# Batched windowed attention with two feed-forward layers on one core: the corner of the v block buffer is cleared by an operation of its own, all band masks are added by TensorE, and the order table is new

## The chip, the cores and the metric

One core of one Trainium2 chip runs the whole program. The metric is the device time of one execution in microseconds (us). TensorE (PE in the profile, with PEld for its weight loads) multiplies matrices; VectorE (DVE), ScalarE (ACT) and GpSimd (POOL) do the elementwise work; SyncE (SP) issues nearly all transfers. Each engine takes its own instructions in the order in which the program lists them.

## What is computed

Attention over 4 batches, 8 heads, 576 positions and 64 columns: a path on inputs averaged over 4 positions, and a local path in which a position sees its neighbours at a distance under 4. Their sum, as 2304 tokens of 512 columns, goes through two feed-forward layers.

```python
def _attn_ref(q, k, v):                       # (4, 8, 576, 64) each
    ...
    out_d = sm_attn(q_d, k_d, v_d)            # q, k, v averaged over 4 positions
    out_up = np.repeat(out_d, factor, axis=2)
    mask = np.abs(pos[:, None] - pos[None, :]) < factor
    scores = scale * np.matmul(q, k.transpose(0, 1, 3, 2))
    scores = np.where(mask, scores, -1000000000.0)
    ...
    return (out_up + np.matmul(attn, v)).astype(np.float32)

def _moe_ref(x, w_in, w_out):                 # (2304, 512), (512, 2048), (2048, 512)
    h = x @ w_in
    return ((h * np.clip(h + 3.0, 0.0, 6.0) / 6.0) @ w_out).astype(np.float32)

def _moe2_ref(x, w1, w2, w3, w_out):          # three (512, 768), one (768, 512)
    return (np.maximum(np.maximum(x @ w1, x @ w2), x @ w3) @ w_out).astype(np.float32)
```

## The kernel before

**Arithmetic.** Activations and weights are split in two f16 parts (high and low), so that each product is three f16 matmuls. The weights come as 64-bit words. Each quarter of `w_in` and `w_out` (512 x 512) is read in two loads of 1 MB (L1152) into one of two raw buffers, and turned into f32 by one operation on ScalarE (L1124), one on GpSimd (L1126) and one on VectorE (L1129) per chunk; then it is squared and summed for a scale (L1169) and split (L1226 and L1228, for some chunks L1219, L1221 and L1223).

**Stages.** Attention of batch 0 opens the program, while the first quarter of the weights arrives. Then the first layer runs for batches 0 and 1 by quarters (`moe1_h`, L1267, and `moe1_y`, L1305), between the attention of batches 1 to 3. From about 340 us on come batches 2 and 3 of the first layer (L1430, L1521), the second layer's three products (L1842) and its output product (L1951), all with seven products in place of eight per block.

**Local attention of a half batch.** `local_scores` multiplies q and k in 12 blocks of 32 queries by 32 keys (L962), in six operations of 16 small matmuls into two PSUM banks. `soft` takes the softmax. For the pairs (batch, half) in `mask_pe` TensorE first writes the mask into the bank, by one bf16 matmul of an identity with `cap16` for each bank (L947), and VectorE reduces and subtracts straight from PSUM (L999, L1001). For the other pairs VectorE adds the mask (L1004, and L1006 for the edge block) into `sm`, reduces (L1008) and subtracts (L1010, on VectorE or GpSimd). `local_out` multiplies the transposed probabilities `pl` with `vw` (L1036), the block copy of v that `load_vw` fetches in eight transfers (L831), and L1056 adds the averaged path's `od` to make x. x is split by L640 (high, ScalarE) and L1340 (low), and the first layer's matmuls L1267 read it.

**The corner of `vw`.** The first block of batch 0 starts three rows before the first row of v, and the last block of batch 3 ends beyond the last. These blocks are cleared first: `load_vw` issues a GpSimd memset (L816 or L818) in the midst of the SP operation that issues the transfers, so that its place among GpSimd's instructions is the place of this SP operation in the order. The transfer of the shortened block (L824 or L828) waits for it, and on SP's queue all later transfers stand behind.

**Order.** `schedule` takes the operations in the order of a written-out table, `ORDER`: numbers are operations as they were recorded, an asterisk picks the other engine of those that can run on two, and `.1` puts in a warm-up matmul (L2085). The table thus sets each engine's sequence. Nothing else of the planner's constants (`FETCH` among them) is read when the program is built.

Of the kernel before, what the change touches and what calls it, by code (L numbers as in the profile page):

```python
# [64 lines left out]
 'mask_pe': ((0, 1), (1, 1), (2, 1), (3, 1), (3, 0)),  # L65
# [120 lines left out]
0-1 5 22 18 6 72 23 67 222 38 213 4 7 9-10 3 2 11-12 8* 19-20 15 13 74 16 24-26 14 27-28 32 34 33 21 69 29-30  # L186
35-36 43 17 44-45 71 31 37 86 88 98 87 89 46 75 99 76 100 77-78 47 79 48 93 90-91 39 92 94 80-81 101 95 68* 392
70* 49-50 73* 41 96* 97* 82-83 55-56 51 57-58 214 227 216 52* 105 219 231 103 40 102 226 110 113 160-161 104 223
215 111 59 115* 162 106-107 53 84 112* 218 109 119 108* 163 54 60 85 217 220 228 165 114 166 121* 120 167 164
224-225 116-117 122 172 61 118 62-64 168 229 221 173 247 123 65* 124 66 248 169 140 139 845 42 230 236 233 170  # L190
141 249-250 174-175 179 251-255 184 186 142 177 185 235 232 125 127 256 126 257 269 176 237 239 234 846 143-144
391 270 128 178 271 180 129 171 130 145 187 132 243 240 275 241 135 131 244-245 242 272 397 150-151 181 238 276
.1 246 188 146 189 258 136* 259 182* 183* 134 260 190 393 403 133 193 287 394 844 399 192* 194 191 137 147 273
398 152 195 261 395 859 262-266 196 402 197 267-268 278 280 198 274 138 400 295 288 281 296 148 289 297 149 847
282 153-154 290 285 283 401 291 408 155 277 279 156 298 860 405 292 157 299-300 404 303-304 293 158* 305 396 159
406 306-307 301 861 848 286 294* 199 862 201 849 308 311-312 200 313-314 409 309 540 302* 315 284 850-851 539
202-203 316 310* 410 317 319 856 852 320-321 863 853 209 318 322 210 .1 339 323 204-206 407 411 855 541 412 854
542 347 340 207 324-325 348 326-327 208 413 858 211-212 329 857 414 341 349 415-418 342 419-422 328 343-344 350
865 868 351 345 864 423 352 870 355-356 334 357-358 363 330 424 335-336 331-332 364-365 346 867 926 366 425 543
353 426 428 866 359 869 429 874-875 333 360 354* 433-436 427 928 927 929 361 367-368 877 545 337 371-372 441 930  # L200
437 906 871 442 932 338 551 369 547 876 362* 438-439 546 933 872 430 550 370* 908 548 907 449-450 443-444 451
445 878 452 376 373 377 556 912 931 934 873 374 431 453 552 375 544 935 446-447 882-887 936* 910* 894 888-889
895 440 457 378-379 381-382 458-460 432 890 380 553 448* 549 454 909 461 386-387 938 891* 950 383-384 487-489
896 462 940 939 455 941 456* 937* 952 554 880 879 557-558 897 388 490 943 495-497 944 892 385 945 491 953 498
389 942 463 898 559 946-947 899 492 390 499 464* 949* 948* 560 465 1000 466 493 951 555 471 893 503 472 500 1002
900-901 1001 1003-1005 501 561 902* 511 904 955 473-474 467-468 512 502* 913* 504 494* 562 505 513 506 1006 469
954 1007 903 563-565 475 911 905 507 980-981 566-572 508 1008 956 958* 509 573 914 477-479 959 480 1476 881 482
# [141 lines left out]
class Plan:  # L349
# [66 lines left out]
def kernel(  # L416
# [73 lines left out]
    T = {}  # L490
# [1635 lines left out]
```

## Time and profile before

| | |
|---|---|
| Median of 3 runs | 780.24 us (779.95 to 783.92) |
| Profiled execution | 780.03 us |
| Its span in the trace | 778.2 us |
| TensorE busy | 737.7 us, 95% of the span |
| VectorE, ScalarE, GpSimd busy | 564.5, 467.8 and 294.2 us |
| Transfers | 68.43 MB |

The profiled execution lies 1.83 us above its own span, and 0.21 us under the median. The page's strip of 40 slices shows TensorE at five to seven tenths in the first three slices (some 58 us), seven in the sixth, and nine in nearly all others; the granted clock falls to five and six tenths in the second and third slice. A share of busy time says little here: what counts is the front of the program, where TensorE waits, and which wait ends last there.

### The profile page before, as it was taken

How to read it: one execution, taken by the hardware profiler on the slowest of the kernel's cores; microseconds unless marked ns; L12 is line 12 of the kernel's file. 1: busy time of each engine (PE TensorE's matmuls, PEld its weight loads, DVE VectorE, ACT ScalarE, POOL GpSimd, SP SyncE). 2: the span in 40 equal slices, each digit the busy share in tenths (PEclk: the TensorE clock that was granted, in tenths of full speed). 3: DMA queues.
4: the chain of work that ended last, by engine and by line, in shares of the span. 5: the costliest groups of instructions: out<-in, count | busy, mean ns of one | idle time of the engine just before them, and what ended most of it. 6: DMA issues, size and time to landing. Idle time of an engine off the chain costs nothing.

```text
span 778.2 us, 20629 instructions
## 1 busy us (share of the span) xinstructions
PE 737.7 (95%) x8493; PEld 552.5 (71%) x8493; DVE 564.5 (73%) x1151; ACT 467.8 (60%) x1067; POOL 294.2 (38%) x325
## 2 busy tenths in 40 slices
PE   5658979999999999999999999999999999999998
PEld 4456756877777787777777777775556766676667
DVE  2959958767876678878954688469999558953793
ACT  5658859776656644549964687369826432633153
POOL 5636345557534223554232122123665402400060
PEclk9658999999999999999999999999999999999999
DMA  9495746741544000004566433204100100010002
GB/s 293 75 271 185 188 118 134 227 99 29 117 92 116 3 3 3 1 21 113 154 165 170 133 108 104 96 5 174 67 1 1 52 4 29 1 41 1 28 15 82
DMA packets 81248, 68.43 MB, mean 88 GB/s; under 512 B 56962, under 2 KB 68226, under 8 KB 81154
## 3 DMA queue, kind: packets, MB, share of 16 engines
q1 hardware_dynamic: 81154, 67.12, 30.8%
q8 instruction: 66, 1.08, 0.6%
q14 instruction: 28, 0.23, 0.1%
HBM read 56.10 MB, written 11.01 MB: 86 GB/s over the span
## 4 chain that ended last, share of the span: by engine, by line
PE 76%; DVE 4%; ACT 2%; issue 2%; POOL 1%; DVEq 0%; POOLq 0%; ACTq 0%
PE y L1521 12%; PE a L1842 10%; PE y L1842 9%; PE y L1305 8%; PE h L1267 8%; PE at L1951 7%; PE a L1430 6%; PE h L1842 3%; PE y L1430 3%; PE at L1036 2%; PE h L1430 2%; PE a L962 1%; PE at L922 1%; PE at L760 1%; PE a L1951 1%
## 5 line engine op out<-in xcount | busy, mean ns | idle before, releaser
L1267 PE MATMUL h<-x,wi 128*128 128x288 f16 x768 | 116.0, 290 | 2.7 <-DVE gf L1282 2.4
L1305 PE MATMUL y<-g,wo 128*128 128x288 f16 x768 | 114.1, 288 | 1.6 <-ACT y L1316 1.3
L1842 PEld LDWEIGHTS <-m2ow 128*128 128x128 f16 x756 | 73.9, 98 | 50.3 <-issue 2.0
L1521 PE MATMUL y<-ga,wo 128*128 128x288 f16 x768 | 96.9, 286 | 0.0
L1267 PEld LDWEIGHTS <-wi 128*128 128x128 f16 x768 | 73.5, 99 | 23.1 <-issue 4.0
L1305 PEld LDWEIGHTS <-wo 128*128 128x128 f16 x768 | 73.7, 98 | 21.5 <-issue 2.9
L1521 PEld LDWEIGHTS <-wo 128*128 128x128 f16 x768 | 75.0, 98 | 19.1
L1287 POOL TENSOR_TENSOR g<-gf,g 128x288 f16<-128x288 f32 x38 | 33.0, 870 | 59.4 <-ACT g L1285 56.7
L1842 PEld LDWEIGHTS <-m2w 128*128 128x128 f16 x378 | 36.9, 98 | 22.2
L1126 POOL TENSOR_SCALAR z<-z 128x384 int32<-128x384 uint32 (+1 forms) x36 | 22.5, 626 | 69.1 <-DMA z<-in_moe_w_dram 29.7
L1842 PE MATMUL a<-yb,m2ow 128*128 128x384 f16 x234 | 42.9, 326 | 1.6 <-DVE a L1852 0.9
L1430 PEld LDWEIGHTS <-S 128*128 128x128 f16 x384 | 37.5, 98 | 9.4
L1842 PE MATMUL y<-yb,m2ow 128*128 128x384 f16 x234 | 43.1, 326 | 0.0
L1129 DVE SCALAR_TENSOR_TENSOR zo<-zo,z 128x384 int32<-128x384 int32 (+1 forms) x36 | 22.9, 639 | 22.1 <-ACT zo L1124 10.8
L1285 ACT CAST g<-gf 128x288 f16<-128x288 f32 x64 | 27.0, 427 | 15.6 <-DVE gf L1282 14.7
L1951 PEld LDWEIGHTS <-hm 128*128 128x128 f16 x324 | 31.7, 98 | 6.1 <-issue 0.6
L1951 PE MATMUL at<-m2fw,hm 128*128 128x256 f16 x288 | 35.2, 272 | 0.7 <-DVE sc L626 0.3
L1430 PEld LDWEIGHTS <-wi 128*128 128x128 f16 x288 | 28.2, 98 | 7.1
L760 PE MATMUL at<-ident,stg 128*128 128x128 f32 x128 | 21.7, 313 | 8.2 <-DVE which L555 5.6
L1126 POOL TENSOR_SCALAR y<-y 128x1024 int32<-128x1024 uint32 (+1 forms) x20 | 22.3, 1114 | 18.0 <-DMA y<-in_moe_w_out_dram 15.4
L1430 PE MATMUL a<-x,S 128*128 128x288 f16 x192 | 28.6, 286 | 0.0
L1430 PE MATMUL y<-x,S 128*128 128x288 f16 x192 | 28.3, 286 | 0.0
(331 smaller groups left out, 1779.5 us busy)
## 6 DMA issues: line engine op xcount, KB each, us to landing
z<-in_moe_w_dram SPq DMA_DIRECT2D x24, 384.0 KB, 3.5
y<-in_moe_w_in_dram SPq DMA_DIRECT2D x8, 1024.0 KB, 6.0
y<-in_moe_w_out_dram SPq DMA_DIRECT2D x8, 1024.0 KB, 5.1
vw<-in_v_dram SPq DMA_DIRECT2D x62, 96.0 KB, 3.6
out_dram<-y SPq DMA_DIRECT2D x18, 256.0 KB, 2.1
stg<-in_k_dram SPq DMA_DIRECT2D x6, 512.0 KB, 6.8
stg<-in_q_dram SPq DMA_DIRECT2D x6, 512.0 KB, 5.7
stg<-in_v_dram SPq DMA_DIRECT2D x6, 512.0 KB, 3.9
```

The costliest lines, as they stand in the source:

```text
L760: nc.tensor.transpose(out=po[:, i, :, f], in_=T[n(f"{nm}{kc}{c // 2}")][:, f, 2 * (c % 2):2 * (c % 2) + 2, :], identity=ident[0:nr, 0:nr])
L1036: nc.tensor.matmul(out=T[pts[cc]][64 * hl:64 * hl + 64, i * QB:i * QB + QB], lhsT=T[n(f"vw{half}")][32 * c:32 * c + 32, i, hl, :], rhs=T[n ...
L1126: op("POOL", c_f32(n), prio, lambda: nc.gpsimd.tensor_scalar(out=words()[0], in0=words()[0].bitcast(U32), scalar1=0.8735 * 2.0 ** -29, sca ...
L1129: op("DVE", c_dve(n), prio, lambda: nc.vector.scalar_tensor_tensor(out=dst().bitcast(I32), in0=dst().bitcast(I32), scalar=3, in1=words()[0 ...
L1267: nc.tensor.matmul(out=hp(), lhsT=T[wt][:, a, kk, i * P:i * P + P], rhs=T[x16][:, e, kk, :], start=(kk == 0 and (a, e) == (0, 0)), stop=(k ...
L1285: op("ACT", c_act(CH, 0, False), prio + LEAD, lambda: nc.scalar.copy(out=T[g16][:, 0], in_=T[gf]), r=[gf], w=[(g16, 0)], new=[buf(g16, "ac ...
L1287: op("DVE", c_dve(CH), prio + LEAD, lambda e: e.tensor_tensor(out=T[g16][:, 1], in0=T[gf], in1=T[g16][:, 0], op=ALU.subtract), r=[gf, (g16 ...
L1305: nc.tensor.matmul(out=T[acc][:, 0:CH], lhsT=T[wt][:, a, i, d * P:d * P + P], rhs=T[gs[i]][:, e], start=(i == 0 and (a, e) == (0, 0)), sto ...
L1430: nc.tensor.matmul(out=ps_(x)(), lhsT=lhs(a, kt), rhs=T[xn][:, e, kt, :], start=(first and kt == 0 and (a, e) == (0, 0)), stop=(kt == 1 an ...
L1521: nc.tensor.matmul(out=T[acc][:, 0:CH], lhsT=T[wt][:, a, 2 * fb + i, d * P:d * P + P], rhs=hl[:, e * S + half * CH:e * S + half * CH + CH] ...
L1842: nc.tensor.matmul(out=b(to), lhsT=w_op(nm, o)[:, a, kt, fp * P:fp * P + P], rhs=T[f"yb{p}{y}"][:, e, kt, :], start=(first and kt == 0 and ...
L1951: nc.tensor.matmul(out=ps_(x)(), lhsT=h_op(p, fp, o)[:, a, i * P:i * P + P], rhs=T["m2wo"][:, j, e, fp, :], start=(first and fp == 0 and ( ...
```

## The change

- `load_vw`: the memset becomes a GpSimd operation of its own (L835 in the changed file), recorded ahead of the SP operation, which now waits for it as for any other. In the table it can thus stand anywhere ahead of the transfers. Lines after it move by two (L962 becomes L964, L1036 L1038, L1152 L1154, L1267 L1269).
- `mask_pe` holds all eight pairs; before it held five. New are half 0 of batches 0, 1 and 2. In half 0 of a masked pair, eight small score matmuls fall away (of 104), since no block overlaps its neighbour.
- `ORDER` is a new table. The numbers of the operations shift with the new ones, so nearly every row of it differs.
- `FETCH` is changed, but is not read.

```diff
- 'mask_pe': ((0, 1), (1, 1), (2, 1), (3, 1), (3, 0)),
+ 'mask_pe': tuple((b, h) for b in range(4) for h in range(2)),
...
-0-1 5 22 18 6 72 23 67 222 38 213 4 7 9-10 3 2 11-12 8* 19-20 15 13 74 16 24-26 14 27-28 32 34 33 21 69 29-30
...
+0-1 5 4 7* 11 9 42 3 12 10 18 22 6 69 23 19-21 64 8 210 15 38 24 219 43 16 25 13-14 29 2 31-32 136 34 30 26 33
...
-    FETCH = ((30.0, 6.0), (45.0, 4.2), (112.0, 3.6), (1e9, 3.0))
+    FETCH = ((30.0, 6.5), (45.0, 5.0), (130.0, 4.6), (1e9, 3.4))
...
-                if b == 0 and half == 0:
-                    nc.gpsimd.memset(vw[0:32, 0, 0, :], 0.0)
-                if b == B - 1 and half == 1:
-                    nc.gpsimd.memset(vw[96:128, 11, 1, :], 0.0)
...
-            op("SP", 6.0, prio, go, w=[t], new=[buf(t, "attn", f"vw{half}", [P, 12, 2, D])])
+            new, r = [buf(t, "attn", f"vw{half}", [P, 12, 2, D])], []
+            if (b, half) in ((0, 0), (B - 1, 1)):
+                r = [(t, "pad")]
+                op("POOL", 0.1, prio, lambda: nc.gpsimd.memset(
+                    T[t][96:128, 11, 1, :] if half else T[t][0:32, 0, 0, :], 0.0), w=r, new=new)
+                new = []
+            op("SP", 6.0, prio, go, r=r, w=[t], new=new)
```

Over the program the counts that change are few: TensorE gains six mask matmuls and loses 24 small score matmuls; VectorE loses six L1004, six L1006, six L1008 and two L1010, and GpSimd four L1010, for six L999 and six L1001 on VectorE. Of the low parts of g (L1287) 34 in place of 26 are on VectorE.

**SP's queue, from the first w_in loads to the first w_out loads.** `y_` is a raw weight buffer, `vw_561` is half 1 and `vw_572` half 0 of batch 0's block copy, `stg` batch 1's k. Before:

```order
L1152 DMA y_154<-in_moe_w_in_dram 128x2x512
L831 DMA vw_561<-in_v_dram 32x12x64 x8
L704 DMA stg<-in_k_dram 128x16x64
L824 DMA vw_572<-in_v_dram 29x64
L831 DMA vw_572<-in_v_dram 32x11x64
L831 DMA vw_572<-in_v_dram 32x12x64 x7
L1152 DMA y_583<-in_moe_w_out_dram 128x2x512
L1152 DMA y_698<-in_moe_w_out_dram 128x2x512
```

After, `vw_155` is half 0 and `vw_232` half 1:

```order
L1154 DMA y_199<-in_moe_w_in_dram 128x2x512
L820 DMA vw_155<-in_v_dram 29x64
L827 DMA vw_155<-in_v_dram 32x11x64
L827 DMA vw_155<-in_v_dram 32x12x64 x7
L827 DMA vw_232<-in_v_dram 32x12x64 x8
L1154 DMA y_539<-in_moe_w_out_dram 128x2x512
L1154 DMA y_590<-in_moe_w_out_dram 128x2x512
L704 DMA stg<-in_k_dram 128x16x64
```

Half 0 now comes first, ahead of half 1, and batch 1's k moves from between the halves to behind the w_out loads.

**GpSimd, the memset.** `pd` and `sm` are probabilities of the two paths, `qkd` the averaged q and k. Before:

```order
L881 TENSOR_TENSOR pd<-pd,dsm 72x288
L1126 TENSOR_SCALAR y_150<-y_150 128x512
L1019 TENSOR_TENSOR sm<-sm,mx 128x384
L816 MEMSET vw_572 32x64
L1126 TENSOR_SCALAR y_583<-y_583 128x512 x2
L1126 TENSOR_SCALAR y_698<-y_698 128x512 x2
```

After:

```order
L741 MEMSET qT 128x4x8
L742 MEMSET kT 128x4x3
L743 MEMSET kT 128x4x5
L835 MEMSET vw_155 32x64
L796 TENSOR_TENSOR qkd<-kT 128x2x2x16
```

The memset moves from behind the softmax of half 0 to the end of the constants.

**TensorE, from the first output blocks of the local path to the last.** `h<-pl,vw` is `local_out` of batch 0, half 0, 48 matmuls for each pair of heads' columns. Before:

```order
L1036 MATMUL h<-pl,vw_572 64x24 x48
L962 MATMUL y<-kT,qT 32x32 x32
L1036 MATMUL h<-pl,vw_572 64x24 x16
L962 MATMUL y<-kT,qT 32x32 x16
L891 MATMUL at<-ident,pd 128x72 x2
L893 MATMUL at<-ident,pd 32x72
L1036 MATMUL h<-pl,vw_572 64x24 x32
L2085 MATMUL h<-warm 128x224
```

After:

```order
L1038 MATMUL h<-pl,vw_155 64x24 x32
L615 MATMUL at<-tiny,ones 128x1
L1038 MATMUL h<-pl,vw_155 64x24 x16
L949 LDWEIGHTS id_85
L949 MATMUL y<-cap_84,id_85 128x384
L949 LDWEIGHTS id_85
L949 MATMUL y<-cap_84,id_85 128x384
L964 MATMUL y<-kT,qT 32x32 x48
L893 MATMUL at<-ident,pd 128x72 x2
L895 MATMUL at<-ident,pd 32x72
L964 MATMUL y<-kT,qT 32x32 x16
L893 MATMUL at<-ident,pd 128x72 x2
```

The first 48 output blocks now stand ahead of the masks and scores of half 1 (`y<-kT,qT`) instead of among them; the warm-up matmul that stood behind the last of them stands ahead of this piece.

## Rows read from the trace of the kernel before

**Rows 1.** Page, busy us (share of the span) xinstructions.
```profile
PE 737.7 (95%) x8493; PEld 552.5 (71%) x8493; DVE 564.5 (73%) x1151; ACT 467.8 (60%) x1067; POOL 294.2 (38%) x325
```

**Rows 2.** By stretch: busy us (count) per engine, PEclk, DMA share, GB/s.
```profile
20.00:40.00 20.00, 13.66 (x260) 9.41 (x257) 18.08 (x53) 13.25 (x49) 11.69 (x15) 0.62 0.47 74
40.00:60.00 20.00, 12.07 (x338) 9.48 (x337) 11.32 (x30) 11.08 (x27) 7.42 (x11) 0.50 0.90 269
```

**Rows 3.** By stretch, longer ones, same columns.
```profile
140.00:340.00 200.00, 196.93 (x3465) 156.68 (x3464) 150.91 (x356) 120.68 (x318) 94.95 (x110) 1.00 0.27 62
...
540.00:600.00 60.00, 58.44 (x362) 35.17 (x361) 57.87 (x96) 36.60 (x62) 33.30 (x21) 1.00 0.08 27
```

**Rows 4.** SP's waits, 0 to 140 us: in total, times, longest.
```profile
SPq L824 <- POOL vw L816: 15.1, 1, 15.1
```

**Rows 5.** Timeline of SP: start, us, what; transfers by line.
```profile
10.40 10.34 SPq L831 DMA_DIRECT2D vw<-in_v_dram  x8
...
36.72 0.30 SPq L824 DMA_DIRECT2D vw<-in_v_dram  x1
...
41.95 0.93 SPq L1152 DMA_DIRECT2D y<-in_moe_w_out_dram  x2
```

**Rows 6.** Timeline of GpSimd: start, us, what, count, [idle before <-releaser].
```profile
4.45 0.12 POOL L743 MEMSET kT<- 128x20 f32 x1
...
36.52 0.17 POOL L816 MEMSET vw<- 32x64 f32 x1
47.56 1.88 POOL L1126 TENSOR_SCALAR y<-y 128x512 int32<-128x512 uint32 x2 [10.87 <-DMA y<-in_moe_w_out_dram]
```

**Rows 7.** Timeline of TensorE, front of the program.
```profile
43.94 2.76 PE L1036 MATMUL h<-pl,vw 32*64 32x24 f32 x94 [2.82 <-DMA vw<-in_v_dram]
...
51.31 1.55 PE L1036 MATMUL h<-pl,vw 32*64 32x24 f32 x32 [3.78 <-DVE x L1056]
...
63.03 3.40 PE L1267 MATMUL h<-x,wi 128*128 128x288 f16 x15
```

**Rows 8.** Timeline of VectorE, front of the program.
```profile
25.28 0.56 DVE L1004 TENSOR_TENSOR sm<-y,cap 128x384 f32<-128x384 f32 x1
...
32.31 2.48 DVE L1129 SCALAR_TENSOR_TENSOR wi<-wi,y 128x512 int32<-128x512 int32 x4
...
48.24 0.69 DVE L1129 SCALAR_TENSOR_TENSOR wo<-wo,y 128x512 int32<-128x512 int32 x1 [7.08 <-POOL y L1126]
...
50.74 0.51 DVE L1056 SCALAR_TENSOR_TENSOR x<-h,sc,od 128x288 f32<-128x288 f32 x1
```

**Rows 9.** TensorE's waits over the span: in total, times, longest.
```profile
PE a L962 <- issue: 6.2, 3, 4.4
```

**Rows 10.** Timeline of TensorE around a long wait for nothing shown.
```profile
101.08 1.51 PE L962 MATMUL a<-kT,qT 64*32 64x32 f32 x154
107.03 0.80 PE L962 MATMUL a<-kT,qT 64*32 64x32 f32 x54 [4.44 <-issue]
```

**Rows 11.** Timeline of TensorE, two such waits that follow.
```profile
166.42 1.08 PE L962 MATMUL a<-kT,qT 64*32 64x32 f32 x103 [1.04 <-issue]
...
169.37 0.59 PE L922 MATMUL at<-pT,vd 128*64 128x72 f32 x10
170.33 0.47 PE L922 MATMUL at<-pT,vd 128*64 128x72 f32 x6 [0.38 <-issue]
```

**Rows 12.** Page, DMA queues: packets, MB, share.
```profile
q8 instruction: 66, 1.08, 0.6%
```

**Rows 13.** Timeline of TensorE: mask matmuls, and expert matmuls at full clock.
```profile
37.66 0.84 PE L947 MATMUL y<-cap,id 128*128 128x384 bf16 x2
...
96.44 2.38 PE L1267 MATMUL h<-x,wi 128*128 128x288 f16 x18
...
127.69 0.50 PE L947 MATMUL a<-cap,id 128*128 128x384 bf16 x2
```

**Rows 14.** By stretch around 65 us, columns as in Rows 2.
```profile
67.00:68.00 1.00, 0.98 (x9) 0.65 (x8) 0.93 (x3) 0.96 (x4) 0.72 (x1) 1.00 0.83 201
```

More of the change, by code (lines that the diff above doesn't have):

```diff
@@ L185 @@
 ORDER = """
-0-1 5 22 18 6 72 23 67 222 38 213 4 7 9-10 3 2 11-12 8* 19-20 15 13 74 16 24-26 14 27-28 32 34 33 21 69 29-30
[L187 to L205, printed above, removed]
@@ new lines @@
+2118-2119 2218 2215 2441 2114 2442 2144 2130 2443 2145 2150 2223 2120 2220 2149 2134 2138 2135 2444 2154
+2151-2152 2214 2224 2226 2136 2225 2133 2140 2147 2155 2153 2221 2139 2450-2451 2445 2452 2156 2453 2446 2227
+2222 2141 2228 2230-2231 2233 2229 2142 2237-2238 2240 2137 2143 2157-2158 2232 2161 2234 2163 2159 2236 2162
+2454-2455 2244 2164 2160 2235 2165-2166 2456 2447 2239 2245 2247 2517 2241 2448 2457 2521 2242 2449 2243 2246
+2252 2248 2251 1467 1413 2458 2253 2250 2519 2249 2522 2254 2258-2259 2261 2260 2255 2523 2525 2262 2460-2464
@@ new lines @@
+2381 2666 2696-2697 2669 2686 2385 2671 2387 2386 2701 2699 2687 2672 2685 2720 2383 2388 2688 2702 2721 2706
+2722 2391 2689* 2690 2703 2691 2389 2420 2382 2704 2390 2398 2392 2707 2693 2394 2692 2694 2705 2709 2421 2393
+2695 2399 2401 2723-2724 2710 2395 2708 2728-2730 2713 2715 2725 2711 2422 2712 2714 2400 2731-2734 2402
+2716-2718 2726 2423 2735 2403 2396 2727 2397 2405 2404 2412 2736 2406-2408 2831 2424 2409 2413 2415 2410 2414
+2416 2411 2417-2418 2738-2740 2747-2748 2741 2749-2751 2742 2752 2743-2746 2795 2836 2796 2801 2832* 2803 2833
@@ new lines @@
+2834* 2425-2426 2516 2430 2835 2838 2427-2428 2737 2429 2840 2839 2753 2797 3229 2754 2799 2755 2841 2757 2804
+2758-2761 2842-2844 2798 2802 2809 2805 2762-2764 2766 2800 2765 2767 3230 2768 2807 2806 2808 2845 2776
+2810-2812 2777 2769-2771 2778 2846-2847 2849 3231 2850 2779 3232 2813 2853 2780 2772-2774 2781-2783 2814 2848
+2815-2817 2756 2851 2785-2792 2818* 2784 2819 2431 2837 2820 2854 3233 2432 2934 2937 3234 2821 3235-3237 2855
+2935 2943 2775 2433-2434 2822 2940 2936 3240 2939 2793 3241 2794 2435 2865 2952 2856-2857 2950 2852 2436-2437
@@ new lines @@
+2858 2876 2859 2877* 2861 2860 2886 2862 2890 2863 2438-2439 2938 2942 2941 2944 2864 2887 2947 2891 2968
+2945-2946 2948-2949 2951 2874 2953 2956 2440 2959 2955 2966 2875* 2954 3551 2870 2957 2878 2866 2879 2961
+2880-2881 2867 2882 2894 2872 2868 2958 2960 2967 2888 2895* 2984 2970 2975 2871 2889 2963 2873 2883 2962 2965
+2884 2969 3001 2892 2964 2971 2982-2983 2885 2972-2973 2893* 2991 2974 2976-2977 2896 2995 2986 2978 2869 2898
+2979 2897* 2985 2899 2980 2988 3002 2900 2981 2908 2999 2987 2909 2989 2901* 2904 2993 2910 2912 2911 2914 3000
@@ new lines @@
+3147-3149 3130-3131 3123 3132-3133 3150 3152-3153 3155-3156 3134-3135 3157 3154 3159-3160 3136 3158 3137
+3164-3166 3161 3557-3558 3560 3162 3167 3297 3169-3170 3559 3171 3173-3175 3172 3563 3163 3168 3177-3179 3176
+3565 3180-3183 3185-3186 3184 3187 3280 3188 3292 3189-3191 3194-3197 3323 3192 3199-3201 3203-3204 3202
+3205-3206 3561-3562 3207-3213 3215-3217 3214 3218-3220 3224 3282 3567 3286 3285 3221 3225-3227 3284 3287 3291
+3293-3294 3304 3295-3296 3564 3298 3305 3299 3301 3313 3307-3308 3302 3310 3300 3317 3569 3309 3303 3311-3312
@@ L346 @@
+3822 3797 3771* 3826 3801 3798 3802 3827 3831-3832 3750* 3778 3780 3751 3779 3799 3781 3828 3803 3800 3833 3752
+3773 3784 3783 3804 3785-3786 3829 3805-3808 3834 3809-3810 3814-3816 3787 3811-3813 3839-3840 3817 3841 3830
+3842 3849-3851 3835-3837 3853-3855 3838 3844-3845 3852 3857 3856 3858-3863 3865 3818 3866-3867 3846 3864 3869
+3847 3868 3843 3848 3870-3878
 """
```

270 lines of the change are left out of this document (130 added, 140 removed).

## The prediction

> **What bounds the kernel now.** The reading starts with the busy times: TensorE is busy for 737.7 of 778.2 us [rows 1], so 40.5 us of idle time, plus what the half clock costs, is all that an order can win without less work. The stretches say where it lies. From 20 to 60 us TensorE is busy for 13.66 and 12.07 of 20 us, at a granted clock of 0.62 and 0.50 [rows 2]; that is 14.3 us. From 140 to 340 us it is idle for 3.1 us, and from 540 to 600 us for 1.6 us, with VectorE at 57.87 of 60 [rows 3]. So the front decides.
>
> There, one chain ends last. SP's queue stood for 15.1 us on the memset of the corner of `vw` [rows 4]: from 21.6 to 36.72 us, when the first transfer of half 0 left; the w_out loads, two places behind, left at 41.95 [rows 5]. GpSimd ran the memset at 36.52, though it had finished the constants at 4.57 (L743), and its next weight operation then waited 10.87 us for w_out [rows 6]. TensorE's local output stood from 41.12 to 43.94 for the `vw` transfer, a wait of 2.82, and its second part 3.78 us for VectorE's L1056 [rows 7]. VectorE reached that L1056 only at 50.74, because the w_out conversions L1129 stand ahead of it and waited 7.08 us [rows 8]. All of this is the same late queue, seen three times; only the last wait on the path counts, so the three are not added up. The expert matmuls' first long run begins at 63.03 [rows 7].
>
> **The change part by part.** *The memset.* Right behind L743 it runs at about 4.6 us, long before SP comes to it. Both halves' v transfers then fall in the time in which SP stood, and the w_out loads wait only for their raw buffers, which the four L1129 of w_in empty from 32.31 to 34.79 [rows 8]. They leave between 32.2 (first buffer emptied early) and 34.8 us in place of 41.95: 7.2 to 9.8 us earlier. Does the rest of the front follow? The local output's other inputs were there by 41.12, and it takes 2.76 us [rows 7], so its first part ends by 43.9 at the latest, and earlier now that it stands ahead of half 1's scores. L1056 can then run at 42 to 44 in place of 50.74: 6.8 to 8.7 us earlier. The splits of x and of w_in behind it keep their lengths. I take **-8** for the start of the long run. If another queue is as late, only TensorE's own 2.8 us go; the ends are -2.8 and -9.8. Half 0 now comes first on SP, where half 1's eight transfers took 10.34 us among the other loads [rows 5], so half 0 lands some 15 us before it is read. Batch 1's k, which moves behind the w_out loads, is not read before the long run, whose start ends its cover.
>
> *The new order around scores.* TensorE waited 6.2 us in three pieces, 4.4 the longest, for nothing that the profile shows ahead of the small score matmuls [rows 9]. The longest came after 154 of 208 such records in one run [rows 10]. Two later ones, at 166.42 and 170.33, have 128 matmul records between them (103, 12, 3 and 10 in four rows, the first and the last shown [rows 11]), and as many weight loads: 256 instructions. The instruction queue moved 1.08 MB in 66 packets, 16.4 KB each [rows 12]. I read these as waits for the next block of instructions, and dense small matmuls use up a block faster than the next one comes. In the new order the run of 104 score matmuls of batch 1, half 0 (two records each) is cut in two of 48 with fifteen expert matmuls between them, which at 132 ns each (2.38 us for 18 [rows 13]) lengthen the block by 2.0 us; the wait should shrink by as much. Elsewhere runs of 64 remain. I take **-2**; the ends are 0 and the whole -6.2.
>
> [...]
>
> *The masks.* Three more pairs of mask matmuls cost 0.84 us at the half clock (batch 0) and 0.50 each at the full one [rows 13], 1.84 in all. Of the small score matmuls 24 go, 48 records at 1.51 / 154 = 9.8 ns [rows 10], 0.47. TensorE's work grows by 1.4 us; the pair in the front partly lies beside waits, so **+1** (0 to +1.4). VectorE loses additions of 0.56 us (L1004 [rows 8]); behind the front these lie beside a busy TensorE and are worth nothing there. In the front they pull the w_in conversions ahead a little, which is in the span of 7.2 to 9.8.
>
> *Everything else that moved.* The low parts of g and the like change engines, and nearly each row has a new place. No row prices that. The idle time after 140 us in the two stretches is 3.1 + 1.6 = 4.7 us [rows 3], the most that could be won; as much may be lost. Value 0, ends -4.7 and +4.7.
>
> The sum: 780.03 - 8 - 2 + 1 + 0 = **771.0 us**. The profiled execution lies 0.2 us under the median, which changes nothing.
>
> **The rivals.** *The waits are not fetches.* Then cutting up the scores leaves them as they are, and the term is 0: 773.0 us. For it: the profile names no releaser. Against it: the spacing of 256. [...]
>
> *Another wait takes the place.* ScalarE and VectorE take their rows in order, and if a conversion or the half clock's small matmuls end as late as the queue did, only 2.8 us of the front go, and the dense front waits for instructions in its turn (no -2): 780.03 - 2.8 + 1 = 778.2 us, no change that can be told. For it: half 1's scores and outputs, some 190 small matmuls, now come back to back, and each block of instructions may then cost a wait like the 4.44. Against it: from 20 to 60 us TensorE ran 598 matmul records and 594 weight loads [rows 2], 4.7 blocks, which at 4.44 + 1.26 us each (the long wait and about what TensorE worked on that block) are 27 us of the 40.
>
> [...]
>
> *More is won.* Front at -9.8 and all of the 6.2: 780.03 - 9.8 - 6.2 + 1 = 765.0.
>
> **How the numbers follow.** The forecast, 771 give or take 4, has 0.54; waits that are not fetches 0.13; another wait 0.20; the slower clock 0.07; more won 0.06. A measurement of this kernel can tell about 0.5%, 3.9 us: faster means under 776.3, slower above 784.1. The forecast, the first and the last rival are faster, 0.73; another wait is no change, 0.20; 0.07 is slower. The range runs from 766 to 778.5: it takes in the forecast with its ends, the first rival and most of "another wait", and leaves out the slower clock and part of the ends.
>
> **What would show it.** Right: SP has no wait on GpSimd in the front; the w_out loads leave at 32 to 35 us; VectorE's wait ahead of the first w_out conversion is under 2 us; the first long run of expert matmuls begins at 54 to 57 us; TensorE's waits for nothing shown ahead of score matmuls sum to about 4 us, none near 4.4; TensorE is busy for about 739 us. Wrong in the front: the w_out loads leave early and the long run still begins after 60. Wrong in the second term: the waits keep their sum. Wrong in the last: TensorE idles for over 8 us after 140 us.

## The result and the profile after

The changed kernel takes 771.73 us (median of four, 769.71 to 773.87) against 780.41 for the kernel before (779.95 to 783.92): a ratio of 0.9876, 95% interval 0.9854 to 0.9898 (9.7 us by the ratio, 8.7 by the medians). The prediction was 771.0 us with 766 to 778.5. The profiled execution is the slowest of the four: 773.87 us, span 772.1. The total thus came out as forecast; the three terms that make it up did not, as the experiments show.

The page's busy time of each engine ([rows 1] before):

```profile
PE 734.2 (95%) x8451; PEld 550.4 (71%) x8451; DVE 557.0 (72%) x1142; ACT 472.4 (61%) x1079; POOL 280.9 (36%) x316
```

The stretches of [rows 2, 3]: length, busy us (count) of PE, PEld, DVE, ACT and POOL, granted clock, DMA share, GB/s:

```profile
40.00:60.00 20.00, 14.44 (x369) 11.33 (x364) 15.39 (x41) 14.58 (x31) 11.43 (x14) 0.50 0.73 196
...
140.00:340.00 200.00, 197.06 (x3455) 156.72 (x3454) 150.82 (x349) 120.05 (x320) 89.80 (x104) 1.00 0.21 52
...
540.00:600.00 60.00, 56.83 (x354) 34.41 (x352) 59.36 (x97) 34.36 (x62) 30.36 (x20) 1.00 0.02 8
```

The queue did what was forecast. SP's timeline (start, length, line; [rows 5]) has no wait for GpSimd ([rows 4]); the v transfers of both halves leave early, and the w_out loads at 32.84 us in place of 41.95:

```profile
12.22 17.55 SPq L827 DMA_DIRECT2D vw<-in_v_dram  x16
32.84 2.38 SPq L1154 DMA_DIRECT2D y<-in_moe_w_out_dram  x2
```

VectorE's timeline ([rows 8]) shows the step behind it: no wait ahead of the first w_out conversion (L1131), and the first L1058 (L1056 before) at 42.91 in place of 50.74. But its second pair begins only at 53.05:

```profile
40.95 2.04 DVE L1131 SCALAR_TENSOR_TENSOR wo<-wo,y 128x512 int32<-128x512 int32 x2
42.91 0.93 DVE L1058 SCALAR_TENSOR_TENSOR x<-h,sc,od 128x288 f32<-128x288 f32 x2
...
53.05 0.52 DVE L1058 SCALAR_TENSOR_TENSOR x<-h,sc,od 128x288 f32<-128x288 f32 x1 [0.71 <-PE h L1038]
```

Before, the second pair began at 57.66:

```profile
57.66 0.50 DVE L1056 SCALAR_TENSOR_TENSOR x<-h,sc,od 128x288 f32<-128x288 f32 x1
```

So the first pair comes 7.8 us earlier, the second only 4.6, and the long run moves like the second.

What stands between is on TensorE's timeline (start, length, line, shapes, count of records, idle time ahead and what ended it; [rows 7]), after half 1's masks:

```profile
26.00 0.45 PE L964 MATMUL y<-kT,qT 64*24 64x32 f32 x31 [3.78 <-issue]
...
41.24 0.81 PE L964 MATMUL y<-kT,qT 64*32 64x32 f32 x55
44.30 0.69 PE L964 MATMUL y<-kT,qT 64*32 64x32 f32 x41 [2.25 <-issue]
44.92 0.50 PE L893 MATMUL at<-ident,pd 72*128 72x72 f32 x2
45.22 0.32 PE L895 MATMUL at<-ident,pd 72*32 72x72 f32 x1
45.47 0.47 PE L964 MATMUL y<-kT,qT 64*32 64x32 f32 x32
45.87 0.50 PE L893 MATMUL at<-ident,pd 72*128 72x72 f32 x2
46.16 0.32 PE L895 MATMUL at<-ident,pd 72*32 72x72 f32 x1
46.42 0.76 PE L964 MATMUL y<-kT,qT 64*32 64x32 f32 x49
49.94 0.36 PE L964 MATMUL y<-kT,qT 64*32 64x32 f32 x15 [2.77 <-issue]
...
59.14 3.09 PE L1269 MATMUL h<-x,wi 128*128 128x288 f16 x12
```

The rows from 44.30 us to the wait that ends at 49.94 hold 41 + 2 + 1 + 32 + 2 + 1 + 49 = 128 records, with their loads 256 instructions: one block in 5.64 us, of which 2.77 were waited. The long run begins at 59.14, 3.9 us earlier than before, not at 54 to 57. TensorE's waits by line (in total, times, longest; [rows 9]) say the same: the waits for nothing shown have nearly left the a bank of batches 1 to 3, where they were 6.2 us, and stand in the front (the y bank), where they were 0.6. Ahead of score matmuls they sum to 9.7 us, where the forecast was about 4:

```profile
PE y L964 <- issue: 8.8, 3, 3.8
...
PE a L964 <- issue: 0.9, 3, 0.5
```

### The profile page after: what moved, and what is told of

It is laid out like the page before. It is cut to its first block, busy times and chain, and to the rows that moved or that the text cites. A ratio compares the mean times of both kernels' runs of the same rounds, so it can differ in the third digit from the quotient of the medians.

```text
span 772.1 us, 20559 instructions
## 1 busy us (share of the span) xinstructions
PE 734.2 (95%) x8451; PEld 550.4 (71%) x8451; DVE 557.0 (72%) x1142; ACT 472.4 (61%) x1079; POOL 280.9 (36%) x316
## 4 chain that ended last, share of the span: by engine, by line
PE 80%; DVE 10%; ACT 3%; DMA 3%; issue 3%; SPq 1%; DVEq 0%; ACTq 0%
PE y L1523 12%; PE y L1307 11%; PE h L1269 10%; PE a L1844 8%; PE y L1844 8%; PE at L1953 7%; PE a L1432 6%; PE y L1432 3%; PE h L1844 3%; PE at L1038 2%; DMA y<-in_moe_w_in_dram 2%; PE h L1432 2%; PE at L924 1%; PE a L964 1%; DMA wi<-in_k_dram 1%
## 5 line engine op out<-in xcount | busy, mean ns | idle before, releaser
L1269 PE MATMUL h<-x,wi 128*128 128x288 f16 x768 | 118.0, 292 | 1.1 <-DVE gf L1284 1.1
L1269 PEld LDWEIGHTS <-wi 128*128 128x128 f16 x768 | 74.6, 100 | 22.2 <-issue 2.6
L1289 POOL TENSOR_TENSOR g<-gf,g 128x288 f16<-128x288 f32 x30 | 23.5, 785 | 55.0 <-ACT g L1287 54.8
L1131 DVE SCALAR_TENSOR_TENSOR zo<-zo,z 128x384 int32<-128x384 int32 (+1 forms) x36 | 18.7, 520 | 24.5 <-ACT zo L1126 23.0
L1287 ACT CAST g<-gf 128x288 f16<-128x288 f32 x64 | 26.9, 428 | 7.6 <-DVE gf L1284 5.9
L1280 ACT ACTIVATE r<-h,sc 128x288 f32<-128x288 f32 x32 | 18.7, 588 | 19.2 <-PE h L1269 19.0
L1342 POOL TENSOR_TENSOR m2fw<-hm 128x384 f32<-128x384 f32 x9 | 9.4, 1048 | 56.9 <-DVE hm L1858 56.4
```

The lines of the kernel that those rows point to most:

```text
L1131: op("DVE", c_dve(n), prio, lambda: nc.vector.scalar_tensor_tensor(out=dst().bitcast(I32), in0=dst().bitcast(I32), scalar=3, in1=words()[0 ...
L1269: nc.tensor.matmul(out=hp(), lhsT=T[wt][:, a, kk, i * P:i * P + P], rhs=T[x16][:, e, kk, :], start=(kk == 0 and (a, e) == (0, 0)), stop=(k ...
L1280: op("ACT", c_act(CH, 2), prio + LEAD, lambda: nc.scalar.activation(out=T[r_], in_=hp(), func=AF.Relu, scale=col(INVH + 4 * b + g), bias=c ...
L1287: op("ACT", c_act(CH, 0, False), prio + LEAD, lambda: nc.scalar.copy(out=T[g16][:, 0], in_=T[gf]), r=[gf], w=[(g16, 0)], new=[buf(g16, "ac ...
L1289: op("DVE", c_dve(CH), prio + LEAD, lambda e: e.tensor_tensor(out=T[g16][:, 1], in0=T[gf], in1=T[g16][:, 0], op=ALU.subtract), r=[gf, (g16 ...
```

## The experiments

Each ratio is to the kernel before, run on the same chip beside it. The changed kernel was measured once, four executions against four, so a difference to it carries the intervals of both ratios. A shorter or longer table shifts the lines: L957, L1031 and L1262 in the kernel with the memset alone are L964, L1038 and L1269 of the changed one; L954, L1028 and L1259 in those with the masks alone or the scores cut are L962, L1036 and L1267 of before. "Long run" is the first long run of expert matmuls in the profiled execution.

| kernel | ratio, 95% interval | long run | span |
|---|---|---|---|
| before | 1 | 63.03 | 778.2 |
| memset alone | 0.9947 (0.9928 to 0.9965) | 61.65 | 777.2 |
| masks alone | 0.9965 (0.9948 to 0.9982) | 62.66 | 776.7 |
| masks alone, padded | 0.9997 (0.9984 to 1.0010) | | 779.9 |
| scores cut | 0.9994 (0.9976 to 1.0012) | 62.34 | 778.5 |
| changed, memset late | 0.9933 (0.9909 to 0.9958) | 61.97 | 776.5 |
| changed, without the masks | 0.9957 (0.9937 to 0.9977) | 62.59 | 777.5 |
| changed | 0.9876 (0.9854 to 0.9898) | 59.14 | 772.1 |
| changed, blocks shifted | 0.9892 (0.9846 to 0.9938) | 61.00 | 778.4 |
| changed, local output first | 0.9899 (0.9870 to 0.9928) | 56.90 | 770.4 |
| changed, mixed | 0.9997 (0.9974 to 1.0019) | 70.60 | 778.1 |

### The memset alone

The kernel before, with its own order; the memset of batch 0 is recorded ahead of the SP operation and stands behind the constants (later numbers shift by one).

```diff
-0-1 5 22 18 6 72 23 67 222 38 213 4 7 9-10 3 2
+0-1 5 22 18 6 73 23 68 223 38 214 4 42 7 9-10 3 2
...
-                if b == 0 and half == 0:
-                    nc.gpsimd.memset(vw[0:32, 0, 0, :], 0.0)
```

> The kernel before with one thing changed: the memset of the corner of batch 0's half-0 vw tile is a GpSimd operation of its own, right behind the constants of the first operation (L741 to L743). All other operations keep their row; half 1's eight v transfers still stand ahead of half 0's on SP. Theory of the prediction (one late queue, seen three times): SP loses its 15.1 us wait, the w_out loads leave near 33 us in place of 41.95, VectorE's 7.08 us wait ahead of the first w_out conversion shrinks to under 2, and the long run of expert matmuls begins 3 to 8 us earlier than 63.03; time 772 to 777 us. Theory from the trace after (dense small matmuls are paced by waits for instruction blocks): the same early loads, but the waits for nothing shown ahead of small matmuls between 20 and 60 us grow from 0.6 to several us, and the long run begins 2.8 to 4.5 us earlier; time 775.5 to 777.5. Rival (hidden anyway): under 1 us, 779 to 781.

Measured: 0.9947, 4.1 us of 780.4 (2.7 to 5.6). The w_out loads left at 34.53 and VectorE's wait fell to 0.59 us, yet the long run began only 1.4 us earlier, less than either of the first two theories had it. TensorE's timeline of this kernel, at the places of [rows 7]:

```profile
41.63 1.47 PE L1031 MATMUL h<-pl,vw 32*64 32x24 f32 x42
44.81 1.69 PE L1031 MATMUL h<-pl,vw 32*64 32x24 f32 x54 [1.71 <-issue]
46.43 0.89 PE L957 MATMUL y<-kT,qT 64*32 64x32 f32 x64
47.25 0.77 PE L1031 MATMUL h<-pl,vw 32*64 32x24 f32 x9
51.77 0.85 PE L1031 MATMUL h<-pl,vw 32*64 32x24 f32 x23 [3.74 <-issue]
```

The waits of 2.82 us for vw and 3.78 for L1056 are gone, and waits for nothing shown of 1.71 and 3.74 have come at nearly the same places, 127 recorded records apart (54 + 64 + 9). In the old order the rival "another wait takes the place" is what happened in the front.

### The memset late, in the new order

The changed kernel; the memset goes behind GpSimd's softmax product (62), half 1's transfers (136) go ahead of half 0's (43).

```diff
-0-1 5 4 7* 11 9 42 3 12 10 18 22 6 69 23 19-21 64 8 210 15 38 24 219 43 16 25 13-14 29 2 31-32 136 34
+0-1 5 4 7* 11 9 3 12 10 18 22 6 69 23 19-21 64 8 210 15 38 24 219 136 16 25 13-14 29 2 31-32 34
...
-62* 161
+62* 42-43 161
```

> The changed kernel with one thing undone: the memset stands behind GpSimd's softmax product of half 0, and half 1's v transfers stand ahead of half 0's on SP, as in the kernel before. Theory of the prediction (the queue decides): SP waits for the memset until about 35.5 us, the w_out loads leave at 40 to 42 us in place of 32.84, TensorE waits some 5 us for the vw transfer, and the long run begins 4 to 9 us later than 59.14; time 776 to 781. Theory that instruction blocks pace the front: part of the delay lies beside waits for blocks (8.8 us in the changed kernel's front), since a TensorE that stands for vw collects a block meanwhile: the long run begins 2 to 5 us later, time 774 to 777, and the waits for nothing shown ahead of batch 0's small matmuls fall below 5 us.

Measured: 0.9933. SP waited 12.3 us for the memset, the w_out loads left at 39.41, TensorE waited 0.74 and 3.54 us for vw, and the long run began at 61.97, 2.8 us later. The waits ahead of the y bank's scores were 5.8 us in place of 8.8: here a TensorE that stood for vw for 4.28 us waited 3.0 us less for blocks. By the ratio the time is 775.2 us of 780.4. That and the long run are as the second theory had them; its mark of waits below 5 us was missed by 0.8, and the first theory's 4 to 9 us for the long run did not come. Against the changed kernel the memset (with the order of v's halves) is worth 0.0057, 4.4 us (give or take 2.6, from both intervals), about half of the 8 of the forecast.

### Are the waits blocks of instructions?

The changed kernel with 16 tiny matmuls behind the first warm-up matmul:

```diff
+        warmed.append(0)
+        for _ in range(16 if len(warmed) == 1 else 0):
+            nc.tensor.matmul(out=T["tail"][0:32, CH:CH + 24], lhsT=warm[0:32, 0:32], rhs=warm[0:32, 0:24],
+                             start=True, stop=True)
```

> The changed kernel with 16 tiny matmuls (32 records, 64 instructions of TensorE with their weight loads) behind the first warm-up matmul near 31 us, where TensorE has room; the results go to unused columns. Theory that the waits for nothing shown in the front are waits for the next block of 256 instructions: the wait at 26.00 us stays where it is, and the two later ones move 32 records ahead: the one at 44.30, behind 55 records of half 1's scores, comes behind about 23, and the one at 49.94, behind 49 records of the last piece, behind about 17. Rival (the waits belong to the matmuls ahead of which they stand, for a bank or for data): they stay behind 55 and 49 records. Time within 1.5 us of the changed kernel's by both.

TensorE's timeline of this kernel, the same rows as above:

```profile
40.42 0.43 PE L964 MATMUL y<-kT,qT 64*32 64x32 f32 x23
42.89 1.02 PE L964 MATMUL y<-kT,qT 64*32 64x32 f32 x73 [2.04 <-issue]
...
45.34 0.37 PE L964 MATMUL y<-kT,qT 64*32 64x32 f32 x17
49.09 0.74 PE L964 MATMUL y<-kT,qT 64*32 64x32 f32 x47 [3.38 <-issue]
49.76 2.34 PE L1038 MATMUL h<-pl,vw 32*64 32x24 f32 x80
54.95 0.64 PE L1038 MATMUL h<-pl,vw 32*64 32x24 f32 x16 [2.84 <-issue]
```

The waits stand behind 23 and 17 records in place of 55 and 49, each 32 records earlier, ahead of matmuls that had waited for nothing. A wait that belonged to a bank or to data would have stayed. A third boundary now falls into L1038 and costs 2.84 us. The two blocks took 6.20 and 5.86 us. The ratio cannot be told from the changed kernel's. The profiled execution, the slowest of six with a span of 778.4 us, also has a wait of 2.31 us at 252.53 that the changed kernel's does not have; that where the boundaries fall is worth some us by itself is suggested by this, not shown.

What the waits are for can be read from the traces directly, which hold the packets of the instruction queue ([rows 12]) one by one. The changed kernel's wait from 47.18 to 49.94 us has one in it (a row of its DMA view for this stretch):

```profile
q8 instruction: 1, 0.02, 2.2%
```

It left at 47.52 and had landed at 48.49, and TensorE went on 1.45 us later. It is the same everywhere. In the 14 traces there are 69 waits for nothing shown of over 0.4 us. All of them stand at the same place modulo 256, within one, when TensorE's recorded instructions (matmuls, weight loads and semaphore operations) are counted from the start (193 or 194 stand ahead in the traces before and after), and each ended 1.3 to 1.7 us after a packet of 16,384 bytes on that queue had landed. So they are waits for the next block of instructions. The releaser that a view names can hide one: the changed kernel's wait of 2.19 us that ends at 124.24, put down to VectorE's L1001, stands at such a place behind 128 score records in one run and ended 1.5 us after a packet.

### A run of scores cut in two

The kernel before; three of the six score operations of batch 1, half 0 (882 to 887) go ahead.

```diff
-376 373 377 556 912 931 934 873 374 431 453 552 375 544 935 446-447 882-887
+376 882-884 373 377 556 912 931 934 873 374 431 453 552 375 544 935 446-447 885-887
```

> The kernel before with one thing changed: three of the six score operations of batch 1, half 0 stand twelve expert matmuls earlier, so the run of 104 score matmuls is cut in two. Theory that the waits for nothing shown are waits for the next block of instructions: the 4.4 us wait near 107 us falls to 0 to 2.5 us, the sum of such waits ahead of a<-kT,qT from 6.2 to 2 to 4.5, and the time to 776.5 to 779. Rival (the waits are not fetches): the sum stays at 6 to 6.5 us and the time within 779.5 to 781.

TensorE's timeline, to be read beside [rows 10]:

```profile
99.24 1.36 PE L954 MATMUL a<-kT,qT 64*32 64x32 f32 x96
100.54 1.28 PE L1297 MATMUL y<-g,wo 128*128 128x288 f16 x9
101.74 0.71 PE L954 MATMUL a<-kT,qT 64*32 64x32 f32 x58
106.22 0.80 PE L954 MATMUL a<-kT,qT 64*32 64x32 f32 x54 [3.77 <-issue]
```

The wait still comes behind the 154th record (96 + 58), since as many instructions stand ahead as before; nine expert matmuls, not twelve, came between, 1.28 us of work, and the wait fell by 0.67, not by 2 to 4.4. The time did not move (0.9994), and the sum of these waits, 5.7 us, lies between the two expectations: the place speaks for blocks, and the size says that here a short pause in a block shortened its wait by less than the pause. The packets show why: the next block's packet left 3.99 us after this block began, where it was 3.34 in the kernel before, and the block took 6.44 us in place of 5.83. Of the 1.28 us of work, 0.61 went into the longer block, and 0.67 is left. The second step of the prediction, that fifteen expert matmuls (2.0 us) would shorten the wait by as much, is not borne out by this run.

### The masks

The kernel before with all masks by TensorE, and the same kernel padded to the old number of small matmuls:

```diff
- 'mask_pe': ((0, 1), (1, 1), (2, 1), (3, 1), (3, 0)),
+ 'mask_pe': tuple((b, h) for b in range(4) for h in range(2)),
...
                 if on_pe and j == 0:
+                    for hl in range(2 if not half and b < 3 else 0):
+                        for c in range(4):
+                            nc.tensor.matmul(
+                                out=T[names[hl]][32 * c:32 * c + 32, 384:416],
...
                     mask()
```

> The kernel before with one thing changed: all eight pairs' masks are added by TensorE. Reduction and subtraction of the three new pairs stand where VectorE's two additions stood; every other operation keeps its row. Prediction's term: TensorE's work +1.4 us (1.84 for six mask matmuls, 0.47 less for 24 small score matmuls), some of it beside waits: 780.4 to 781.8 us. Rival: fewer small matmuls move the boundaries of instruction blocks, and VectorE's shorter way in the front lets the first softmax end about 1 us earlier, so the time falls: 777 to 780.

> The kernel with the masks alone, and eight small matmuls into unused columns ahead of each of the three new masks, so that TensorE has as many small matmuls as in the kernel before. Theory that the masks gain because 32 instructions fewer per pair shorten the waits for blocks: 32/256 of a block of 5.6 us, 0.7 us for each of the three pairs, so the time is 1.5 to 2.5 us over that with the masks alone, 780.5 to 782 where the kernel before has 782. Theory that they gain by less work on VectorE and GpSimd: within 1 us of the masks alone, 778.5 to 780.3.

Measured: 0.9965 with the masks alone, a gain of 2.7 us (1.4 to 4.1) where the prediction had a loss of 1, and 0.9997 when padded: 24 small matmuls, 0.47 us of work, cost 2.5 us (give or take 1.7). TensorE's waits for nothing shown from 140 to 340 us, first with the masks alone:

```profile
PE a L954 <- issue: 1.6, 2, 1.3
```

and padded:

```profile
PE y L1304 <- issue: 2.5, 2, 1.4
PE a L961 <- issue: 1.1, 1, 1.1
```

With the padding, waits for nothing shown appear ahead of expert matmuls (L1304), where the kernel without it has none. The padding leaves VectorE's relief as it is and takes the gain back. So in the old order the masks win by fewer small matmuls; whether by their number or by where the block boundaries then fall, these runs do not separate.

The other way round, the changed kernel without the three new masks (both additions and the reduction stand in the reduction's place):

```diff
- 'mask_pe': tuple((b, h) for b in range(4) for h in range(2)),
+ 'mask_pe': ((0, 1), (1, 1), (2, 1), (3, 1), (3, 0)),
```

> The changed kernel with one thing undone: the masks of batches 0 to 2, half 0, are added by VectorE again (both additions and the reduction stand where the reduction stood). Prediction's term for the masks (+1 us): the time falls by 0 to 1.4 us, 770 to 772. Theory from the kernel with the masks alone (-2.7 us there): the time rises by 1.5 to 4 us, 773 to 776; in the front by VectorE's 1.1 us of additions and the longer softmax of half 0.

Measured: 0.9957, 6.3 us (give or take 2.3) slower than the changed kernel, more than either expectation; the long run began at 62.59, 3.5 us later. VectorE's timeline of this kernel has what comes back, L999 and L1001 twice each, and L1051 (L1058 of the changed kernel) 1.67 us later; TensorE's has a further block wait ahead of the transposes:

```profile
26.72 0.56 DVE L999 TENSOR_TENSOR sm<-y,cap 128x384 f32<-128x384 f32 x1 [1.72 <-PE y L957]
27.38 0.19 DVE L1001 TENSOR_TENSOR sm<-y,cap_lo 128x32 f32<-128x32 f32 x1
...
44.58 0.93 DVE L1051 SCALAR_TENSOR_TENSOR x<-h,sc,od 128x288 f32<-128x288 f32 x2
```

```profile
57.57 0.40 PE L886 MATMUL at<-ident,pd 72*128 72x72 f32 x2 [2.63 <-issue]
```

The same boundary cost the changed kernel 0.21 us (at 56.16). Once the queue no longer decides, VectorE's softmax of half 0 is on the path: 2 x (0.56 + 0.19) = 1.5 us of additions are 1.67 us of delay, where the prediction had called them a little in the span of the first term. The profiled executions differ by 5.4 us, and 3.5 of these are there when the long run begins; where the rest comes from was not traced.

### Local output first, and mixed

Two orders of the front, made from what the shifted kernel shows. In the first the second part of half 0's local output stands ahead of half 1's masks and scores, with VectorE's and ScalarE's rows behind it moved along; in the second the first 24 expert matmuls stand in four groups among these scores as well. TensorE's operations, changed, first and mixed (127 to 129 local output, 137 to 142 scores, 181 and 184 transposes, 284 to 295 experts):

```
124 | 137 138 139 181 140 184 141 142 | 127 129 128
124 | 127 129 128 | 137 138 139 181 140 184 141 142
124 | 127 129 128 | 137 138 139 181 284 285 140 184 292 293 141 286 287 142 294 295
```

> The changed kernel with the second part of half 0's local output (L1038, 96 records) ahead of half 1's masks and scores, VectorE's L1058 of half 0 ahead of the w_out conversions, and the splits of x and of the first quarter of w_in close behind; nothing else moves. Theory that half 1's dense scores, two blocks of instructions, are what holds up x after the early memset: x is split some 5 us earlier, and since half 1's scores still stand ahead of the expert matmuls, the long run begins 2 to 5 us earlier than 59.14; time 1 to 4 us under the changed kernel. Rival (the same blocks of instructions come ahead of the long run in either order, so TensorE is late by the same number of blocks): the long run begins within 1.5 us of 59.14, and the time is within 1.5 us.

> As lo_first, and the first 24 expert matmuls stand in four groups between half 1's score operations. Theory that instruction blocks pace the front: expert matmuls (two instructions, 227 ns at the half clock) fill the waits between blocks of small matmuls, so the first 24 expert matmuls (5.4 us at the half clock) cost little: the twentieth expert matmul, at 64.0 us in the changed kernel, comes 4 to 7 us earlier, and the time is 2 to 6 us under the changed kernel. Rival (the front is then late by half 1's softmax and its local output, which come later here): the gain is taken back by 90 us, and the time is within 1.5 us of the changed kernel's.

TensorE's timelines, the first order and then the mixed one:

```profile
40.02 3.19 PE L1031 MATMUL h<-pl,vw 32*64 32x24 f32 x96 [0.94 <-DVE x L1051]
...
56.90 4.46 PE L1262 MATMUL h<-x,wi 128*128 128x288 f16 x18
```

```profile
50.02 1.65 PE L1262 MATMUL h<-x,wi 128*128 128x288 f16 x6
...
70.60 3.04 PE L1262 MATMUL h<-x,wi 128*128 128x288 f16 x12 [3.37 <-DVE gf L1277]
```

The first order brought the long run to 56.90 us and the span to 770.4, but its ratio, 0.9899, cannot be told from that of the shifted kernel measured beside it (0.9892), nor from the changed kernel's (1.8 us more, give or take 2.8). The long run moved as the first theory had it; the fall of 1 to 4 us in time did not come, and the rival's 1.5 us cannot be excluded. With x there earlier, TensorE now waited 2.2 us for VectorE's maximum of the w_out scale (L596) behind half 1's scores. The mixed order began the experts at 50.02 and lost it all: after the first 24 the next ones waited for VectorE's L1277, whose rows had kept their places behind other work, and came at 70.60. The block waits were not filled either (8.0 us ahead of the y bank's scores). It is 7.6 us slower than the first order by the ratios, which neither theory had.

### What a dense block costs by itself

128 small matmuls into unused columns in batch 1's last quarter, in one run, and 16 at a time:

```diff
                 T["tail"] = T[h]
+                if (b, g) == (1, 3):
+                    for _ in range(128 if (half, i) == (0, 0) else 0):
+                        nc.tensor.matmul(out=T[h][0:32, CH:CH + 32], lhsT=warm[0:64, 0:32], rhs=warm[0:64, 0:32],
+                                         start=True, stop=True)
```

> The changed kernel with 128 small f32 matmuls (64x32 by 32 columns, 512 instructions) in one run behind one expert block of batch 1's last quarter, near 310 us, where TensorE is busy nearly throughout; they write unused columns. Their work is 128 x 19.6 ns = 2.5 us (two records of 9.8 ns each). Theory that dense small matmuls are paced by instruction blocks and that one block is there ahead: the run crosses two or three block boundaries, the first is free, each further one costs a wait of 3 to 5 us: the time is 6 to 12 us over the kernel with the same matmuls spread out. Theory of a hidden fetch: 2.5 us over the changed kernel, as when spread out, and no wait for nothing shown.

> The changed kernel with the same 128 small matmuls, 16 behind each of the eight expert blocks of batch 1's last quarter. Both theories: 2 to 3.5 us over the changed kernel, which is their work, and no long wait for nothing shown among them, since expert matmuls stand between. If 512 more instructions cost time wherever they stand, it is as slow as the dense run.

Neither told anything of blocks. The ratios were 0.9986 and 1.0012, which is 8.6 and 10.6 us over the changed kernel's (each give or take 2), and no wait for nothing shown appeared among the added matmuls, because they were not as short as assumed. One row of each timeline:

```profile
304.75 8.29 PE L1276 MATMUL h<-warm 64*32 64x32 f32 x256
```

```profile
307.50 1.20 PE L1276 MATMUL h<-warm 64*32 64x32 f32 x32
```

That is 32 and 37 ns a record in place of 9.8, and a work of 8.29 us and of 8 x 1.20 = 9.6 us, about what they cost. All of them go to one place of the array, while the kernel's scores alternate between eight; the operands differ too, so that this is the reason is a reading, not shown. Two blocks in 8.29 us showed no wait. The next kernel takes 128 of its own score matmuls instead, ahead of the masks of batch 3, half 0:

```diff
+                if (b, half, j) == (3, 0, 0):
+                    for rep in range(16):
+                        for hl in range(2):
+                            for c in range(4):
+                                nc.tensor.matmul(
+                                    out=T[names[hl]][32 * c:32 * c + 32, 0:32],
...
+                                    start=True, stop=True, tile_position=(64 * hl, 32 * c))
                 if on_pe and j == 0:
                     mask()
```

> The changed kernel with 128 more small score matmuls of the kernel's own kind (four column places, two row places, 256 records, 512 instructions) in one run ahead of the masks of batch 3, half 0, near 244 us, which overwrite them. Their work is 256 x 9.8 ns = 2.5 us. Theory of instruction blocks: the run crosses two block boundaries, 128 records apart, so one or two waits for nothing shown appear 128 records apart, each of 2 to 5 us (a block costs 3.5 to 6 us in all, less the 1.26 us of work in it): the time is 5 to 11 us over the changed kernel. Rival (instructions are there in time, and small matmuls cost their work): 2 to 3 us over it, and no wait over 0.6 us.

Its ratio was 0.9988 (0.9961 to 1.0015), 8.7 us over the changed kernel's (give or take 2.7) for 2.5 us of work; the rival's 2 to 3 us is outside. TensorE's timeline of this kernel, and under it the expert matmuls that follow in the changed one:

```profile
241.58 1.09 PE L956 MATMUL a<-kT,qT 64*32 64x32 f32 x104
242.88 1.28 PE L956 MATMUL a<-kT,qT 64*32 64x32 f32 x128 [0.21 <-issue]
246.88 0.44 PE L956 MATMUL a<-kT,qT 64*32 64x32 f32 x24 [2.72 <-issue]
...
249.00 3.09 PE L1278 MATMUL h<-x,wi 128*128 128x288 f16 x12
```

```profile
245.01 1.63 PE L1269 MATMUL h<-x,wi 128*128 128x288 f16 x12
```

One boundary costs 0.21 us, and the next, exactly 128 records on, 2.72: a block that holds 1.28 us of work takes 4.00. The packet for this block had landed at 241.40; the next one left at 244.03, only 1.15 us after the boundary, and landed at 245.48. And there is a second price. The twelve expert matmuls behind it take 3.09 us in place of 1.63, since the granted clock fell: from 240 to 250 us it was 0.81 on average here and 1.00 in the changed kernel, whose twelve at 59.14 us also took 3.09, at 0.50.

## Why the prediction was right, and which steps were wrong

**The reading of the front** was right: SP's 15.1 us wait is gone, the w_out loads leave at 32.84 us (32 to 35 forecast), VectorE does not wait for w_out, L1058 runs at 42.91 (42 to 44).

**The memset's term was mis-sized.** It was -8; the runs give -4.1 in the old order and -4.4 in the new one, between the ends of -2.8 and -9.8. The step that failed is to take the first pair of L1056 for all that the long run needs, with "the splits behind it keep their lengths": the first pair came 7.8 us earlier, as forecast (6.8 to 8.7), the second only 4.6, because the second part of the local output stood behind half 1's scores, and these cost two block waits (2.25 and 2.77 us). I had this as the rival "another wait takes the place" and, in the argument against it, a price of 5.7 us a block (measured 5.64), but gave it 0.20 and did not put it into the sum. The mark "wrong in the front if the long run begins after 60" was not reached; the forecast of 54 to 57 was missed by 2.

**The masks' term had the wrong sign.** It was +1, from the work of 6 matmuls more and 24 fewer. Measured: -2.7 in the old order, -6.3 in the new one. The same prediction that took the waits for blocks of 256 instructions counted the 24 small matmuls by their 9.8 ns a record, though in a dense run 96 instructions are 96/256 of a block that costs 4 to 7 us. And VectorE's additions were on the path once the queue was not, where the prediction let them lie within the first term.

**The order's term** was -2, with one run cut. Its waits did shrink, from 6.2 to 0.9 us, or 3.1 with the one at 124.24, but the cut alone did nothing, and 8.8 us of such waits stand in the front. The step "the wait should shrink by as much" took the length of a block as fixed; it was not. The order as a whole can be read along two ways, in us from the ratios: memset -4.1, order +0.8, masks -6.3; or masks -2.7, order -2.5, memset -4.4; -9.7 each, but for rounding. With some 2 us of uncertainty on each step the order by itself is worth nothing that can be told.

**Everything else that moved** was put at 0. After 140 us the idle time went from 4.7 to 2.9 + 3.2 = 6.1 us in the two stretches, and is under 8. TensorE is busy for 734.2 us and not 739. The records alone (six masks more, 48 small ones fewer) would have added 1.4 us; less time at the lower clock (from 60 to 80 us 0.93 was granted in place of 0.85) goes the right way, but its share was not separated. The slower clock, which had 0.07, did not show: in the changed kernel it was 0.50 from 40 to 60 us, as before, and higher than before from 60 to 80.

So the sum of -9 is -9.7 by the ratios, but by -4, -2.7 to -6, and about nothing, in place of -8, +1 and -2. Two errors of 4 us and more cancelled; that the total fell on the forecast is luck. The price of a block, which the argument had in hand, was left out of both.

The rival "the waits are not fetches" is refuted: the waits moved by 32 records with 64 instructions, a block took 4.00 us for 1.28 us of work, and each wait ended behind a packet of instructions. In the kernel with the added scores the next block's packet left at 244.03 us, while the 128 records from 242.88 to 244.16 still ran, but landed only at 245.48: TensorE waited 2.72 us.

Why a block takes 4.00 us at 244 us and 5.6 to 7.0 in the front can be told in part. From the packet's start to TensorE's next matmul it took 2.3 to 2.9 us in all of them; what differs is how long after the boundary the packet left, 1.15 us at 244 us and 3.09 to 4.43 in the front. The lower clock is not needed for that: in the kernel before, the block that begins behind the 26th of the 154 records of [rows 10], at 101.20, took 5.83 us, and its packet left after 3.34 us, at a granted clock of 1.00. The two stretches from boundary to packet, in the kernel before and in the one with the added scores (columns as in [rows 2]):

```profile
101.20:104.54 3.34, 1.39 (x154) 1.27 (x152) 0.35 (x2) 3.34 (x7) 3.02 (x4) 1.00 0.90 331
```

```profile
242.88:244.03 1.15, 1.15 (x128) 1.15 (x128) 0.45 (x2) 0.00 (x0) 1.09 (x3) 1.00 0.91 197
```

The DMA engines' busy share is the same in both; 331 GB/s moved in one and 197 in the other. What holds the packet back stays open.

## What to carry to other kernels

Count TensorE's small matmuls as instructions, not as work: in a dense run the price is that of a block of 256 instructions (64 f32 matmuls here, 4.00 to 6.96 us), so removing a few of them can pay more than their time (24 fewer, 0.47 us of work, were worth 2.5 us in the old order), and a mask matmul of two instructions is cheap (two of them took 0.50 us [rows 13]). A wait for which the profile names nothing may still have its cause in the trace: count instructions from one such wait to the next, and look for the instruction queue's packets. When one late queue is mended, ask which wait ends last then, and price it in the sum itself, also for terms whose work looks hidden. A sum that comes out right proves its parts no better than one that does not: undo each part alone, in the old order and in the new one.

## What the runs showed of the hardware

- A block of 256 instructions, 128 records with their loads, took 4.00 us at 244 us, 5.64, 5.86 and 6.20 in the fronts of the changed and the shifted kernel, and 6.96 (44.81 to 51.77) with the memset alone. Nine expert matmuls (1.28 us) put into one took only 0.67 us off its wait.
- In these blocks the next block's packet left 1.15 to 4.43 us after the boundary, took 0.9 to 1.5 us, and TensorE went on 1.4 to 1.6 us after it had landed.
- A wait of 2.72 us for a block was followed by the lower clock (0.81 granted from 240 to 250 us): twelve expert matmuls took 3.09 us in place of 1.63.
- f32 matmuls of 64x32 by 32 columns took 9.8 ns a record where they alternated between eight places of the array, and 32 ns in the run in which all went to one.
- The granted clock in the records did not always fit the matmuls' times: in the profiled execution of the kernel with the scores cut it reads 0.995 over the whole span, while fifteen expert matmuls at 62.34 us took 3.78 us, against 3.40 at 63 us in the kernel before [rows 7], where it reads 0.58.
